# Weight loads split in halves, staged LN1 with transposes inside the projection, and a reordered attention-output phase in a fused linear-attention + ReGLU block

## The chip, the cores and the metric

The kernel runs on one core of a Trainium2 chip. The metric is device time in microseconds (us). "PE" is TensorE, "PEld" its weight loads, "DVE" VectorE, "ACT" ScalarE, "POOL" GpSimd, "SP" the sync engine, which here issues most loads. Each run lists the mean clock granted to TensorE over the whole run (1.0 is full speed).

## The reference, cut to what matters

```python
x = A_x                                             # 1 x 2048 x 1024, bf16
# block A: linear attention, 32 heads of 32
qkv = layernorm(x) @ wqkv ; pq, pk = phi(q), phi(k) # phi(t) = t+1 if t>0 else exp(t), + 1e-6
kv = pk^T v ; z = sum(pk)
o  = (pq kv) / (pq z + 1e-6)
h  = x + o @ wo
# block B: gated ReGLU, F = 3584
g  = relu(layernorm(h) @ W_gate) ; h2 = h + (g * (layernorm(h) @ W_up)) @ W_down
```

## The kernel before

All tensors are cut into 16 row tiles (`t`) of 128 rows. Every operation is recorded by a small scheduler, `E(engine, fn, reads, writes)`, which derives semaphore waits from the named buffers; each engine then runs its own list in the order of recording. PSUM has eight banks, handed out least recently used first (`alloc_banks`). The head of the kernel normalises four tiles, transposes each, and projects it with the first quarter of wkv:

```python
load_x(0, 1, halves=True)
load_x(1, 1)
load_wkv(jorder[0], "sp")            # 1 MB, one DMA
for t_ in range(2, 4): load_x(t_, 1)
...
def LN1(t, fast):                    # DVE: bn_stats x2, bn_aggr, +eps ; POOL: rstd = pow(-0.5)
    ...                              # fast: DVE normalises the tile; else POOL does, in two operations
def T1(t, eng="act"):                # 8 PE transposes into one bank, one eviction of 128x1024
    bk = transposes(ln1tile[t % N_L1], b_ln1tile[t % N_L1])
    t_evac(bk, lnT, b_ln1T[t], t, eng)
def KV(t, j):                        # 8 matmuls 128x512, then V's eviction (ACT) or phi (ACT, DVE, DVE)
    ...
for i in range(10):                  # warm-up matmuls on ident and etmp
    E("pe", ... e.matmul(psum[wb][:], lhsT=ident, rhs=etmp[0], ...))
LN1(blk0[0], True)
T1(blk0[0], "dve")
for idx, t in enumerate(blk0):       # the first four tiles
    if idx + 1 < len(blk0):
        LN1(blk0[idx + 1], idx + 1 < 2)
    KV(t, jorder[0])
    if idx + 1 < len(blk0):
        T1(blk0[idx + 1])
```

Later, "phase 4" computes the attention output, the projection with wo and the second layernorm in a software pipeline over tiles:

```python
for i in range(n_iter):
    if i < NT: ND(i)                 # PE: numerators and denominators, 3 banks
                                     # ACT: 3 x denominators + eps; DVE: reciprocal, 3 x normalise
    ... two Q projections while any are left (i < 8) ...
    if 0 <= i - 1 < NT: TO(i - 1)    # PE transposes, ACT eviction
    if 0 <= i - 2 < NT:
        for n in range(DC): A(i - 2, n)   # PE 2 x 8 matmuls; DVE adds the residual (eviction + row sums)
        LN2(i - 2)                   # ACT Square over the tile of h; DVE small; POOL rstd and normalise
    if i >= NT: ... two gate/up tasks GU ...
    if 0 <= i - TL_LAG < NT: TL(i - TL_LAG)  # TL_LAG = 4; PE transposes, ACT eviction
load_wd(); ...                       # then the dense gate/up and down projections, to the end
```

(The second block is shortened to its calls.)

## Time and profile before

| | before |
|---|---|
| time, median of the first 6 runs | 865.8 us (864.47 to 867.95) |
| span of the profiled run, its clock | 863.8 us, 0.998 |
| first useful projection matmul | 9.85 us |
| PE dense from | 21.8 us |
| period of a phase-4 iteration without Q | 5.83 us |
| weight loads waiting for the normalise line | 8.1 us |

From the page of the profiled run, the busy times (us, share of the span, instructions) and the engine shares of the chain that ended last:

```profile
PE 843.2 (98%) x4279; PEld 400.9 (46%) x4362; DVE 278.8 (32%) x541; ACT 193.5 (22%) x337; POOL 62.7 (7%) x101
...
PE 87%; DVE 5%; ACT 4%; DMA 3%; issue 1%; SPq 0%
```

TensorE is the engine that counts. In the timeline eight 128x512 matmuls take 1.727 us when nothing stops them, 0.216 us each; the kernel has 3712 of them, so some 801 us of its 864 cannot be touched by reordering. The Trainium skill (Perfetto Trace Analysis, "Identifying the Most-Contended Engine") warns that matmul busy time is no good measure of the distance to the limit. One must look for stretches in which the matmuls don't follow each other every 0.216 us. There are two.

**The head.** Lines of the timeline of the kernel before (start us, duration us, engine, line, operation, output<-input, count, and in brackets the idle time of the engine before it and what ended it). L502 is the projection, L483 the eviction of a transposed tile on ACT, L509 the eviction of V on ACT:

```profile
9.85 3.32 PE L502 MATMUL ps<-big 128*128 128x512 bf16 x8 [2.74 <-DMA big<-in_A_wqkv_dram]
...
13.21 0.60 ACT L509 ACTIVATE big<-ps 128x512 bf16<-128x512 f32 x1 [10.93 <-PE ps L502]
...
13.70 1.02 ACT L483 ACTIVATE big<-ps 128x1024 bf16<-128x1024 bf16 x1
...
14.78 1.90 PE L502 MATMUL ps<-big 128*128 128x512 bf16 x8 [1.16 <-ACT big L483]
...
18.51 1.67 PE L502 MATMUL ps<-big 128*128 128x512 bf16 x7 [1.38 <-ACT big L483]
...
21.79 8.81 PE L502 MATMUL ps<-big 128*128 128x512 bf16 x39 [1.16 <-ACT big L483]
```

The first projection starts at 9.85 us, when wkv has landed, and needs 3.32 us for eight matmuls. Then PE waits each time for two evictions in a row on ACT (0.60 and 1.02 us), because the next tile is transposed only after the whole projection, and V's eviction is ahead of it in ACT's list. (The line at 18.51 us shows seven matmuls of eight: one record is missing. Its first weight load, at 18.28 us, gives the start, so these tiles follow each other every 3.5 us.) From 21.79 us on the matmuls are dense. Stretches of 1 us of the same trace (length in us, busy PE us, number of matmuls, granted clock, DMA share, GB/s) show why the first eight were slow:

```profile
9.00:10.00 1.00, 0.15 (x1) 0.69 1.07 387
10.00:11.00 1.00, 1.00 (x3) 0.50 1.09 376
11.00:12.00 1.00, 1.00 (x4) 0.50 1.11 367
12.00:13.00 1.00, 1.00 (x4) 0.61 1.06 370
```

The clock fell to half. The warm-up matmuls had ended at 6.2 us and the first tile's transposes at 7.1 us; after that PE was idle.

**Phase 4 without Q.** One turn in the timeline of the kernel before (L564 normalise, L580 eviction of A, L586 Square, L483 eviction of TL's transposes, L552 denominators, L554 reciprocal, all on DVE or ACT; on PE L540 the ND matmuls, L475 the transposes of TO):

```profile
234.34 1.61 DVE L564 TENSOR_TENSOR big<-ps,rden 128x384 bf16<-128x384 f32 x3
...
235.54 0.29 PE L540 MATMUL ps<-big 128*128 128x132 bf16 x2 [0.24 <-DVE big L564]
235.86 0.68 DVE L580 SCALAR_TENSOR_TENSOR big<-ps,big 128x512 bf16<-128x512 f32 x1
...
236.00 0.62 PE L475 MATMUL ps<-big 128*128 128x128 bf16 x8 [0.17 <-DVE big L564]
...
236.47 0.69 DVE L580 SCALAR_TENSOR_TENSOR big<-ps,big 128x512 bf16<-128x512 f32 x1
...
237.20 1.06 ACT L586 ACTIVATE big<-big 128x1024 bf16<-128x1024 bf16 x1 [2.36 <-DVE big L580]
...
238.25 1.00 ACT L483 ACTIVATE big<-ps 128x1024 bf16<-128x1024 bf16 x1
...
239.16 0.59 ACT L552 ACTIVATE deneps<-ps 128x12 f32<-128x12 f32 x3
...
239.78 0.35 DVE L554 RECIPROCAL rden<-deneps 128x32 f32<-128x32 f32 x1 [1.24 <-ACT deneps L552]
...
240.16 1.61 DVE L564 TENSOR_TENSOR big<-ps,rden 128x384 bf16<-128x384 f32 x3
```

Follow the DVE and ACT lines from top to bottom: each starts where the one above ends, and the last is the first one again, 5.82 us later. It is a ring. PE itself needs only 4.8 us per iteration and is held up twice by the normalise (the brackets). The list of waits (us in total, times, longest) has for the weight loads over the whole run:

```profile
PEld ps L540 <- DVE big L564: 4.2, 13, 0.4
...
PEld ps L475 <- DVE big L564: 3.9, 8, 1.5
```

Together 8.1 us. The matmuls' own waits on that line (2.5 + 1.5 us) show only half of it: matmuls are pipelined, and the modelled end of the last one covers a part of the gap.

### The profile page before, as it was taken

To read this page: it belongs to the slowest core of one execution; us is meant where nothing else is said; L and a number is where in the kernel's file an instruction comes from. 1 tells how busy PE (TensorE), PEld (TensorE's weight loads), DVE (VectorE), ACT (ScalarE), POOL (GpSimd) and SP (SyncE) were. 2 spreads that over 40 slices of the span, in tenths; PEclk is the share of its full clock that TensorE was granted. 3 is DMA by queue.
4 is the path that set the end of the run, shared out by engine and by line. 5 is a ranking of instruction groups with operands and counts; after the bars stand their busy time and mean duration, and the time that the engine had idled before them with its cause. 6 is when DMAs were issued, how large, how long until landed. Compare 5 with 4: busy or idle time off the path is not lost.

```text
span 863.8 us, 10251 instructions
## 1 busy us (share of the span) xinstructions
PE 843.2 (98%) x4279; PEld 400.9 (46%) x4362; DVE 278.8 (32%) x541; ACT 193.5 (22%) x337; POOL 62.7 (7%) x101
## 2 busy tenths in 40 slices
PE   6999999999999999999999999999999999999998
PEld 2444446455544444444444444444444444444443
DVE  5465637887665211111112111111221011112101
ACT  2444432344565321100011110001111001111100
POOL 4123100012233000000000000000000000000000
PEclk9999999999999999999999999999999999999999
DMA  9500003700000469930055552025555103553000
GB/s 310 177 1 2 1 1 104 189 1 1 2 1 1 127 198 347 250 107 25 19 152 158 154 154 77 24 61 147 153 159 154 41 25 104 147 146 97 7 19 24
DMA packets 134413, 83.50 MB, mean 97 GB/s; under 512 B 2656, under 2 KB 127840, under 8 KB 134368
## 3 DMA queue, kind: packets, MB, share of 16 engines
q1 hardware_dynamic: 134224, 82.72, 32.4%
q8 instruction: 34, 0.56, 0.3%
q10 hardware_dynamic: 144, 0.13, 0.0%
q14 instruction: 11, 0.09, 0.0%
HBM read 78.64 MB, written 4.19 MB: 96 GB/s over the span
## 4 chain that ended last, share of the span: by engine, by line
PE 87%; DVE 5%; ACT 4%; DMA 3%; issue 1%; SPq 0%
PE ps L740 22%; PE ps L722 21%; PE ps L726 21%; PE ps L502 13%; PE ps L528 5%; DVE big L564 2%; PE ps L576 2%; DMA big<-in_B_W_gate_dram 2%; DVE big L580 2%; ACT big L483 1%; ACT big L586 1%; PE ps L475 1%; DMA big<-in_A_wqkv_dram 1%; PE ps L517 1%; ACT deneps L552 1%
## 5 line engine op out<-in xcount | busy, mean ns | idle before, releaser
L722 PE MATMUL ps<-big 128*128 128x512 bf16 x879 | 210.0, 379 | 1.2 <-DMA big<-in_B_W_gate_dram 0.3
L726 PE MATMUL ps<-big 128*128 128x512 bf16 x878 | 210.1, 379 | 0.9
L740 PE MATMUL ps<-big 128*128 128x512 bf16 x878 | 192.9, 379 | 0.9
L731 DVE TENSOR_TENSOR big<-ps,big 128x512 bf16<-128x512 f32 x112 | 77.4, 691 | 308.4 <-PE ps L726 308.4
L730 ACT ACTIVATE big<-ps 128x512 bf16<-128x512 f32 x112 | 66.8, 597 | 453.1 <-PE ps L722 453.1
L740 PEld LDWEIGHTS ps<-big 128*128 128x128 bf16 x896 | 87.7, 98 | 105.7
L726 PEld LDWEIGHTS ps<-big 128*128 128x128 bf16 x896 | 87.7, 98 | 105.7 <-DMA big<-in_B_W_up_dram 0.3
L722 PEld LDWEIGHTS ps<-big 128*128 128x128 bf16 x896 | 87.5, 98 | 105.5 <-DMA big<-in_B_W_gate_dram 0.8
L502 PE MATMUL ps<-big 128*128 128x512 bf16 x500 | 113.3, 382 | 7.0 <-ACT big L483 3.7
L502 PEld LDWEIGHTS ps<-big 128*128 128x128 bf16 x512 | 49.6, 98 | 64.7 <-ACT big L483 4.0
L744 DVE TENSOR_TENSOR big<-ps,big 128x512 bf16<-128x512 f32 x32 | 22.1, 691 | 171.3 <-PE ps L740 171.3
L494 DVE TENSOR_SCALAR big<-ps 128x512 bf16<-128x512 f32 x64 | 44.1, 689 | 59.1 <-ACT big L493 59.1
L528 PE MATMUL ps<-big 128*128 128x512 bf16 x251 | 56.4, 379 | 0.3
L576 PE MATMUL ps<-big 128*128 128x512 bf16 x243 | 55.9, 379 | 0.7
L493 ACT ACTIVATE big<-ps 128x512 bf16<-128x512 f32 x64 | 38.2, 597 | 68.6 <-PE ps L528 34.8
L483 ACT ACTIVATE big<-ps 128x1024 bf16<-128x1024 bf16 x47 | 47.5, 1015 | 6.3 <-PE ps L475 6.3
L496 DVE SCALAR_TENSOR_TENSOR big<-big 128x512 bf16<-128x512 bf16 x64 | 44.3, 692 | 2.2
L528 PEld LDWEIGHTS ps<-big 128*128 128x128 bf16 x256 | 24.7, 98 | 28.1
L576 PEld LDWEIGHTS ps<-big 128*128 128x128 bf16 x256 | 24.4, 98 | 26.4
L475 PE MATMUL ps<-big 128*128 128x128 bf16 x384 | 29.2, 219 | 2.7 <-DVE big L564 2.5
L475 PEld LDWEIGHTS ps<-big 128*128 128x128 bf16 x384 | 24.6, 98 | 13.8 <-DVE big L564 3.9
L509 ACT ACTIVATE big<-ps 128x512 bf16<-128x512 f32 x32 | 19.2, 599 | 45.2 <-PE ps L502 45.2
(44 smaller groups left out, 232.1 us busy)
## 6 DMA issues: line engine op xcount, KB each, us to landing
big<-in_B_W_gate_dram SPq DMA_DIRECT2D x56, 512.0 KB, 3.9
big<-in_B_W_up_dram SPq DMA_DIRECT2D x56, 512.0 KB, 4.8
big<-in_B_W_down_dram SPq DMA_DIRECT2D x4, 1792.0 KB, 17.2
big<-in_A_wqkv_dram SPq DMA_DIRECT2D x6, 1024.0 KB, 10.9
out_dram<-big SPq DMA_DIRECT2D x32, 128.0 KB, 1.7
big<-in_A_x_dram SPq DMA_DIRECT2D x6, 512.0 KB, 11.1
big<-in_A_wo_dram SPq DMA_DIRECT2D x1, 2048.0 KB, 8.5
big<-in_A_x_dram SPq DMA_DIRECT2D x3, 256.0 KB, 8.2
```

Source lines behind the costliest of these rows:

```text
L475: E("pe", lambda e, k=k: e.transpose(psum_bf[bk][:, k * P:(k + 1) * P], src_ap[:, k * P:(k + 1) * P], ident), reads=[src_buf, b_ident], wr ...
L483: E("act", lambda e: e.activation(dst, src, ACT.Copy), reads=[b_ps[bk]], writes=[dst_buf])
L494: E("dve", lambda e: e.tensor_scalar(ttmp[r], psum[bk][:], 0.0, 1e-6, op0=ALU.max, op1=ALU.add), reads=[b_ps[bk]], writes=[b_ttmp[r]])
L496: E("dve", lambda e: e.scalar_tensor_tensor(dst_ap, etmp[r], 1.0, ttmp[r], op0=ALU.min, op1=ALU.add), reads=[b_etmp[r], b_ttmp[r]], writes ...
L502: E("pe", lambda e, k=k: e.matmul(psum[bk][:], lhsT=lnT[:, k, t * P:(t + 1) * P], rhs=wkv[:, k, j * 512:(j + 1) * 512], start=(k == 0), st ...
L528: E("pe", lambda e, k=k: e.matmul(psum[bk][:], lhsT=wq[:, k, f * P:(f + 1) * P], rhs=lnT[:, k, c * 512:(c + 1) * 512], start=(k == 0), sto ...
L576: E("pe", lambda e, k=k: e.matmul(psum[bk][:], lhsT=oT[:, k, ts_ * P:(ts_ + 1) * P], rhs=wo[:, k, n * 512:(n + 1) * 512], start=(k == 0), ...
L722: E("pe", lambda e, k=k: e.matmul(psum[gb][:], lhsT=wgs[slot][:, k, fo:fo + P], rhs=lnT[:, k, c * 512:(c + 1) * 512], start=(k == 0), stop ...
L726: E("pe", lambda e, k=k: e.matmul(psum[ub][:], lhsT=wus[slot][:, k, fo:fo + P], rhs=lnT[:, k, c * 512:(c + 1) * 512], start=(k == 0), stop ...
L730: E("act", lambda e: e.activation(relu[r], psum[gb][:], ACT.Relu), reads=[b_ps[gb]], writes=[b_relu[r]])
L731: E("dve", lambda e: e.tensor_tensor(hhT[:, f, :], psum[ub][:], relu[r], op=ALU.mult), reads=[b_ps[ub], b_relu[r]], writes=[b_hh[f]])
L740: E("pe", lambda e, f=f: e.matmul(psum[bk][:], lhsT=hhT[:, f, tt * P:(tt + 1) * P], rhs=wd[:, f, n * 512:(n + 1) * 512], start=(f == 0), s ...
```

## The change

Its intent: get PE dense earlier, and take the bubbles out of phase 4. The diff, cut to its core; the lines of phase 4 are written without their range tests:

```diff
-    TL_LAG = 4
+    TL_LAG = 5
+    SQ_LAG = 3
@@ loads: wkv in two DMAs per quarter; x2 and x3 go to ACT's queue
+        KH = 2 if KT >= 2 else 1
+        b_wkv = [[Buf(f"wkv{j}_{h}") for h in range(KH)] for j in range(2 * DC)]
-            load_x(1, 1)
+            load_x(1, 1, q="sp")
+            load_x(2, 1, q="act")
         load_wkv(jorder[0], "sp")
-        for t_ in range(2, min(4, NT)):
-            load_x(t_, 1)
+            load_x(3, 1, q="act")
@@ warm-up: needs only DVE's memset; 12 ahead, 3 after the first transposes
-        NWARM = 10
-              ... e.matmul(psum[wb][:], lhsT=ident, rhs=etmp[0], ...)
+              ... e.matmul(psum[wb][:], lhsT=etmp[0][:, 0:P], rhs=etmp[0], ...)
+        warm(12)
@@ T1(split=True): two banks of four transposes, two ACT evictions; KV(mid=...): calls mid() after four matmuls
-        LN1(blk0[0], True)
-        T1(blk0[0], "dve")
+        ...
+        T1(blk0[0], "act", split=True)
+        warm(3)
         for idx, t in enumerate(blk0):
-            if idx + 1 < len(blk0):
-                LN1(blk0[idx + 1], idx + 1 < 2)
-            KV(t, jorder[0])
-            if idx + 1 < len(blk0):
-                T1(blk0[idx + 1])
+            if nx is not None:
+                for i in range(0 if idx == 0 else 1, DC):
+                    LN1_bn(nx, i)
+                LN1_fin(nx)
+                if nx2 is not None:
+                    LN1_bn(nx2, 0)           # statistics of the tile after next, while POOL computes rstd
+                LN1_norm(nx, True)           # on DVE for all four tiles
+                KV(t, jorder[0], mid=(lambda nx=nx: T1(nx, "act", split=True)))
+            else:
+                KV(t, jorder[0])
@@ phase 4
         for i in range(n_iter):
             ND(i)
-            Q, Q
-            TO(i - 1)
-            A(i - 2, 0); A(i - 2, 1); LN2(i - 2)
-            GU, GU                            # i >= NT
-            TL(i - 4)
+            TL(i - 5)
+            TO(i - 1)
+            Q or GU                           # GU from i >= NT - 1
+            A(i - 2, 0)
+            LN2(i - 3)
+            Q or GU
+            A(i - 2, 1)
```

More of the change, by code (lines that the diff above doesn't have):

```diff
@@ L329, in bass_sequential_preLN__linear_attn_block__glu_gated_reglu__prompt_kernel @@
         b_ln2T = bl("ln2T", NT)
-        b_wkv = bl("wkv", 2 * DC)
+        KH = 2 if KT >= 2 else 1
+        b_wkv = [[Buf(f"wkv{j}_{h}") for h in range(KH)] for j in range(2 * DC)]
         b_wq = bl("wq", DC)
@@ L381, in alloc_banks @@
             return got
+        E("dve", lambda e: e.memset(etmp[0], 0.0), writes=[b_etmp[0]])
         E("pool", lambda e: e.memset(mhalf[:], -0.5), writes=[b_mhalf])
@@ L387, in bass_sequential_preLN__linear_attn_block__glu_gated_reglu__prompt_kernel @@
                                             base=0, channel_multiplier=1), reads=[b_ident], writes=[b_ident])
-        E("pool", lambda e: e.memset(etmp[0], 0.0), writes=[b_etmp[0]])
         E("pool", lambda e: e.memset(vext[:, :, :, 128:129], 1.0), writes=[b_vones])
@@ L394, in bass_sequential_preLN__linear_attn_block__glu_gated_reglu__prompt_kernel, with load_x @@
             E("dve", lambda e, h=h: e.memset(mask4[32 * h:32 * h + 32, h:h + 1], 1.0), writes=[b_mask4])
-        def load_x(t0, m, q="sp", halves=False):
+        def load_x(t0, m, q="sp", halves=False, extra=()):
             if halves:
@@ L402, in load_x, with load_wkv, load_wq @@
                            writes=[b_x[t0][n]])
-                return
+                return None
             s_ = dsem()
             src = x2[t0 * P:(t0 + m) * P, :].rearrange("(t p) d -> p t d", p=P)
-            Sd.dma(q, lambda e: e.dma_start(xh[:, t0:t0 + m, :], src), s_,
-                   writes=[b for t in range(t0, t0 + m) for b in b_x[t]])
-        def load_wkv(j, q="act"):
-            s_ = dsem()
-            src = A_wqkv[:, D + j * 512:D + (j + 1) * 512].rearrange("(k p) n -> p k n", p=P)
-            Sd.dma(q, lambda e: e.dma_start(wkv[:, :, j * 512:(j + 1) * 512], src), s_, writes=[b_wkv[j]])
-        def load_wq(j, q="act"):
+            return Sd.dma(q, lambda e: e.dma_start(xh[:, t0:t0 + m, :], src), s_,
+                          writes=[b for t in range(t0, t0 + m) for b in b_x[t]], extra_waits=list(extra))
+        def load_wkv(j, q="sp", extra=(), halves=None):
+            tk_ = None
+            for h in (range(KH) if halves is None else halves):
+                s_ = dsem()
+                k0, k1 = h * KT // KH, (h + 1) * KT // KH
+                src = A_wqkv[k0 * P:k1 * P, D + j * 512:D + (j + 1) * 512].rearrange("(k p) n -> p k n", p=P)
+                tk_ = Sd.dma(q, lambda e, k0=k0, k1=k1, src=src: e.dma_start(wkv[:, k0:k1, j * 512:(j + 1) * 512], src), s_,
+                             writes=[b_wkv[j][h]], extra_waits=list(extra))
+            return tk_
+        def load_wq(j, q="act", extra=()):
             s_ = dsem()
             src = A_wqkv[:, j * 512:(j + 1) * 512].rearrange("(k p) n -> p k n", p=P)
-            Sd.dma(q, lambda e: e.dma_start(wq[:, :, j * 512:(j + 1) * 512], src), s_, writes=[b_wq[j]])
+            return Sd.dma(q, lambda e: e.dma_start(wq[:, :, j * 512:(j + 1) * 512], src), s_, writes=[b_wq[j]],
+                          extra_waits=list(extra))
         def load_wo(q="sp"):
@@ L428, in bass_sequential_preLN__linear_attn_block__glu_gated_reglu__prompt_kernel @@
         if NT > 1:
-            load_x(1, 1)
+            load_x(1, 1, q="sp")
+        if NT > 2:
+            load_x(2, 1, q="act")
         load_wkv(jorder[0], "sp")
-        for t_ in range(2, min(4, NT)):
-            load_x(t_, 1)
+        if NT > 3:
+            load_x(3, 1, q="act")
         t0 = min(4, NT)
@@ L447, in bass_sequential_preLN__linear_attn_block__glu_gated_reglu__prompt_kernel, with LN1_bn, LN1_fin @@
         phi_ring = Ring([0, 1])
-        def LN1(t, fast):
-            for i in range(DC):
-                E("dve", lambda e, i=i: e.bn_stats(stats1[:, t, i, :], xh[:, t, i * 512:(i + 1) * 512]),
-                  reads=[b_x[t][i]], writes=[b_stats1[t]])
+        def LN1_bn(t, i):
+            E("dve", lambda e: e.bn_stats(stats1[:, t, i, :], xh[:, t, i * 512:(i + 1) * 512]),
+              reads=[b_x[t][i]], writes=[b_stats1[t]])
+        def LN1_fin(t):
             E("dve", lambda e: e.bn_aggr(mv1[:, t, :], stats1[:, t].rearrange("p a b -> p (a b)")),
@@ L458, in LN1, with LN1_norm @@
               reads=[b_veps1[t], b_mhalf], writes=[b_rstd1[t]])
+        def LN1_norm(t, fast):
             r = t % N_L1
@@ L470, in LN1 @@
                   reads=b_x[t] + [b_nmr1[t], b_rstd1[t]], writes=[b_ln1tile[r]])
+        def LN1(t, fast):
+            for i in range(DC):
+                LN1_bn(t, i)
+            LN1_fin(t)
+            LN1_norm(t, fast)
         def transposes(src_ap, src_buf):
@@ L485, in t_evac, with T1 @@
                 E("dve", lambda e: e.tensor_copy(dst, src), reads=[b_ps[bk]], writes=[dst_buf])
-        def T1(t, eng="act"):
-            bk = transposes(ln1tile[t % N_L1], b_ln1tile[t % N_L1])
-            t_evac(bk, lnT, b_ln1T[t], t, eng)
+        def T1(t, eng="act", split=False):
+            src_ap = ln1tile[t % N_L1]
+            src_buf = b_ln1tile[t % N_L1]
+            if not split or KT < 2:
+                bk = transposes(src_ap, src_buf)
+                t_evac(bk, lnT, b_ln1T[t], t, eng)
+                return
+            h = KT // 2
+            for part in range(2):
+                bk = alloc_banks(1)[0]
+                ks = list(range(part * h, (part + 1) * h if part == 0 else KT))
+                for k in ks:
+                    E("pe", lambda e, k=k, bk=bk, k0=ks[0]: e.transpose(psum_bf[bk][:, (k - k0) * P:(k - k0 + 1) * P],
+                                                                        src_ap[:, k * P:(k + 1) * P], ident),
+                      reads=[src_buf, b_ident], writes=[b_ps[bk]], inc=(k == ks[-1]))
+                src = psum_bf[bk][:, 0:len(ks) * P].rearrange("p (k s) -> p k s", k=len(ks))
+                dst = lnT[:, ks[0]:ks[-1] + 1, t * P:(t + 1) * P]
+                E("act", lambda e, src=src, dst=dst: e.activation(dst, src, ACT.Copy), reads=[b_ps[bk]], writes=[b_ln1T[t]])
         def phi_evac(bk, dst_ap, dst_buf):
@@ L497, in phi_evac, with KV @@
               reads=[b_etmp[r], b_ttmp[r]], writes=[dst_buf])
-        def KV(t, j):
+        def KV(t, j, mid=None):
             bk = alloc_banks(1)[0]
             for k in range(KT):
+                if mid is not None and k == KT // 2:
+                    mid()
                 E("pe", lambda e, k=k: e.matmul(psum[bk][:], lhsT=lnT[:, k, t * P:(t + 1) * P],
                                                 rhs=wkv[:, k, j * 512:(j + 1) * 512], start=(k == 0), stop=(k == KT - 1)),
-                  reads=[b_ln1T[t], b_wkv[j]], writes=[b_ps[bk]], inc=(k == KT - 1))
+                  reads=[b_ln1T[t], b_wkv[j][k * KH // KT]], writes=[b_ps[bk]], inc=(k == KT - 1))
             if j < DC:
@@ L616, in bass_sequential_preLN__linear_attn_block__glu_gated_reglu__prompt_kernel, with warm @@
         wb = alloc_banks(1)[0]
-        NWARM = 10
-        for i in range(NWARM):
-            E("pe", lambda e: e.matmul(psum[wb][:], lhsT=ident, rhs=etmp[0], start=True, stop=True),
-              reads=[b_ident, b_etmp[0]], writes=[b_ps[wb]], inc=(i == NWARM - 1))
+        def warm(n):
+            for i in range(n):
+                E("pe", lambda e: e.matmul(psum[wb][:], lhsT=etmp[0][:, 0:P], rhs=etmp[0], start=True, stop=True),
+                  reads=[b_etmp[0]], writes=[b_ps[wb]], inc=(i == n - 1))
+        warm(12)
         NJ = 2 * DC
@@ L625, in bass_sequential_preLN__linear_attn_block__glu_gated_reglu__prompt_kernel @@
         blk0 = blocks[0]
-        LN1(blk0[0], True)
-        T1(blk0[0], "dve")
-        for idx, t in enumerate(blk0):
-            if idx + 1 < len(blk0):
-                LN1(blk0[idx + 1], idx + 1 < 2)
-            KV(t, jorder[0])
-            if idx + 1 < len(blk0):
-                T1(blk0[idx + 1])
+        nb0 = len(blk0)
+        for i in range(DC):
+            LN1_bn(blk0[0], i)
+        LN1_fin(blk0[0])
+        LN1_norm(blk0[0], True)
+        T1(blk0[0], "act", split=True)
+        warm(3)
+        for idx, t in enumerate(blk0):
+            nx = blk0[idx + 1] if idx + 1 < nb0 else None
+            nx2 = blk0[idx + 2] if idx + 2 < nb0 else None
+            if nx is not None:
[8 more added lines that the diff above has]
+                KV(t, jorder[0])
         for b, blk in enumerate(blocks):
@@ L651, in bass_sequential_preLN__linear_attn_block__glu_gated_reglu__prompt_kernel @@
                     T1(t_)
-        handoff(b_wkv, [b for row in b_pq for b in row])
+        handoff([b for row in b_wkv for b in row], [b for row in b_pq for b in row])
         q_tasks = [(f, c) for c in range(NCH) for f in range(KT)]
@@ L693, in bass_sequential_preLN__linear_attn_block__glu_gated_reglu__prompt_kernel @@
             handoff([b_ln1T[t]], [b_ln2T[t]])
-        n_iter = NT + TL_LAG + 1
+        n_iter = NT + max(TL_LAG, SQ_LAG) + 1
         q_rest = len(q_tasks) - qi
@@ L762, in bass_sequential_preLN__linear_attn_block__glu_gated_reglu__prompt_kernel, with q_some, gu_some @@
         gi = 0
+        def q_some(n_):
+            nonlocal qi
+            for _ in range(n_):
+                if qi < len(q_tasks):
+                    Q(*q_tasks[qi])
+                    qi += 1
+        def gu_some(n_):
+            nonlocal gi
+            for _ in range(n_):
+                if gi < len(gu_tasks) and gu_tasks[gi][0] == 0 and all(b_ln2T[t_].written for t_ in range(4)):
+                    GU(*gu_tasks[gi])
+                    gi += 1
         for i in range(n_iter):
+            q_now = q_per_iter if (qi < len(q_tasks) and i < q_iters) else 0
+            g_now = 2 if (i >= NT - 1 and gi < len(gu_tasks) and gu_tasks[gi][0] == 0) else 0
             if i < NT:
                 ND(i)
-            if qi < len(q_tasks) and i < q_iters:
-                for _ in range(q_per_iter):
-                    if qi < len(q_tasks):
-                        Q(*q_tasks[qi])
-                        qi += 1
+            if 0 <= i - TL_LAG < NT:
+                TL(i - TL_LAG)
             if 0 <= i - 1 < NT:
                 TO(i - 1)
+            q_some((q_now + 1) // 2)
+            gu_some((g_now + 1) // 2)
             if 0 <= i - 2 < NT:
-                t = i - 2
-                for n in range(DC):
-                    A(t, n)
-                LN2(t)
-            if i >= NT and gi < len(gu_tasks) and gu_tasks[gi][0] == 0:
-                for _ in range(2):
-                    if gi < len(gu_tasks) and gu_tasks[gi][0] == 0 and all(b_ln2T[t_].written for t_ in range(4)):
-                        GU(*gu_tasks[gi])
-                        gi += 1
-            if 0 <= i - TL_LAG < NT:
-                TL(i - TL_LAG)
+                A(i - 2, 0)
+            if 0 <= i - SQ_LAG < NT:
+                LN2(i - SQ_LAG)
+            q_some(q_now // 2)
+            gu_some(g_now // 2)
+            if 0 <= i - 2 < NT:
+                for n in range(1, DC):
+                    A(i - 2, n)
         while qi < len(q_tasks):
```

## The prediction

> **What bounds it now.** TensorE. The page gives PE 98% busy, PE 87% of the chain that ended last. In the timeline eight 128x512 matmuls pass in 1.727 us (0.216 us each) almost everywhere; 3712 of them are about 801 us, and nothing in the change removes one. Only idle or slow PE time can be won, and it lies in two places.
>
> 1. *Head, 0 to 22 us.* The timeline shows the first useful projection matmuls at 9.85 us, 2.7 us after PE went idle, released by the DMA of wkv (list of waits; 8.0 us in the chain). These eight take 3.3 us instead of 1.73 (granted clock 0.72 at 10-15 us). Then the chain goes round per row tile: matmuls, V eviction on ACT (0.60), transposed-tile eviction on ACT (1.02), next matmuls: starts at 14.78, 18.5, 21.79, about 3.5 us each, PE busy half. Dense from 21.8 us.
> 2. *Phase 4 without Q, 224 to 271 us.* The period is 5.83 us, though PE needs 3.45 (A) + 2x0.44 (transposes) + 0.4 (ND) = 4.73. The ring is DVE normalise (1.5) -> two A evictions (1.35) -> ACT Square (1.05) -> ACT TL eviction (0.9) -> ACT denominators (0.6) -> reciprocal (0.35) -> next normalise. PE's weight loads wait on that normalise 4.2+3.9 = 8.1 us in all (waits); about 0.5 + 6x1.05 + 1.5 us. Iterations with Q have period 8.27 against 8.2 needed: no gain there.
>
> **What changes.** Head: wkv comes in halves; x2, x3 move to ACT's queue; warm-up needs only DVE's memset, is two longer, with three more after the first transposes; tiles 2, 3 are normalised on DVE (0.55) instead of POOL (0.26+1.20); transposes are put into the middle of the preceding projection, so their eviction overlaps its second half, and V's eviction comes after it. Estimate from the durations: first projection at about 8.5 us at full clock, then about 2.75 us per tile (transposes 0.45, eviction 1.25, half a projection 0.86, latencies 0.2): last of the four starts at about 16.7 instead of 21.8. **Gain 5 us (3 to 7)**. The added warm-up costs nothing useful. The skill (TensorE: Matmul & The Clock Gate, "What's actually happening") says that the clock is released after some 3.4 us of activity and lost after an idle window; the slow first eight agree. The skill (DMA: Bandwidth & Descriptors, "Issuing engines are not separate DMA queues") says a second issuer adds no bandwidth, so loads still move at the 330-365 GB/s of 5-15 us and wkv's half cannot come very early.
>
> Phase 4: Square moves one iteration later, after both tile evictions on ACT, so A's last eviction is no longer in the ring. ACT needs about 3.9 us, DVE about 3.8 per iteration, under PE's 4.73. The bubble goes; gate/up work also fills iteration 15 and after. **Gain 8 us (6 to 8.5)**, all on the critical path, as PE runs densely afterwards. The w_down load keeps 14 gate/up tasks (48 us) before its use, against the 26 us it took: no new wait.
>
> **Time:** 865.8 - 5 - 8 = 852.7 us, range 849.5 to 858.0. Faster by over 2% (under 848.5): 0.06; within: 0.93; slower: 0.01.
>
> **What would show it.** Waits of PE weight loads on the normalise line near zero; phase 4 period near 4.75 us; projection dense from 16-17.5 us; clock 1.0 from 8 us; FFN cadence unchanged; the one gate-load wait at 343 us still under 1 us.
>
> **What would make it wrong.** Half of wkv lands no earlier, as the ACT queue's x loads share the engines; x2 late stalls DVE's statistics in front of tile 1's normalise; DVE, now waiting for Square before A's second eviction, holds a PSUM bank (7 of 8 used per iteration) and leaves part of the bubble.

## The result, and the profile after

The changed kernel took 852.12 us (median of 7 runs, 851.83 to 852.56), the kernel before 865.53 us (16 runs, 863.72 to 867.95). The ratio is 0.9846 (95% interval 0.9835 to 0.9858). Here and below a ratio is the mean time of one kernel's fast runs over that of the other's of the same rounds, so it is not quite the ratio of the medians quoted. The gain is 13.4 us, 1.5%: within 2%. The same two lines of the page, after:

```profile
PE 839.5 (99%) x4283; PEld 400.8 (47%) x4367; DVE 282.8 (33%) x543; ACT 195.8 (23%) x342; POOL 59.4 (7%) x96
...
PE 98%; DMA 1%; issue 1%; ACT 0%; SPq 0%; DVE 0%; ACTq 0%
```

PE's busy time hardly moved; the span did, and nearly all of the chain that ended last is now PE.

**The head** in the timeline after (L538 projection, L518 split transposes, L523 their evictions on ACT):

```profile
8.33 1.02 PE L538 MATMUL ps<-big 128*128 128x512 bf16 x4 [0.65 <-DMA big<-in_A_wqkv_dram]
...
9.39 0.62 PE L518 MATMUL ps<-big 128*128 128x128 bf16 x8
...
9.83 1.28 ACT L523 ACTIVATE big<-ps 128x512 bf16<-128x512 bf16 x2 [1.69 <-PE ps L518]
...
9.94 1.02 PE L538 MATMUL ps<-big 128*128 128x512 bf16 x4
...
11.17 1.04 PE L538 MATMUL ps<-big 128*128 128x512 bf16 x4 [0.20 <-ACT big L523]
...
13.80 1.04 PE L538 MATMUL ps<-big 128*128 128x512 bf16 x4 [0.28 <-ACT big L523]
...
16.44 8.81 PE L538 MATMUL ps<-big 128*128 128x512 bf16 x39 [0.28 <-ACT big L523]
```

The first half of the projection starts at 8.33 us and runs at full speed; the next tile's transposes stand between its halves, and ACT evicts them (from 9.83 us) while the second half runs. After the first, the tiles follow each other every 2.64 us, and PE is dense from 16.44 us instead of 21.79: 5.35 us. The first matmuls of phase 4 come by the same 5.34 us earlier, at 162.07 us instead of 167.41 us (first line before, second after):

```profile
167.41 0.63 PE L540 MATMUL ps<-big 128*128 128x132 bf16 x8
162.07 0.63 PE L576 MATMUL ps<-big 128*128 128x132 bf16 x8
```

The granted clock is 1.00 in every stretch from 6 to 17 us; one of them:

```profile
10.00:11.00 1.00, 0.96 (x5) 1.00 1.09 346
```

**Phase 4**, one turn after (on PE L576 ND, L494 the transposes of TL and TO together, L612 A; L588 denominators, L502 the two tile evictions on ACT, L600 normalise, L616 eviction of A, L622 Square):

```profile
228.27 0.63 PE L576 MATMUL ps<-big 128*128 128x132 bf16 x8
...
228.74 1.05 PE L494 MATMUL ps<-big 128*128 128x128 bf16 x16
...
229.43 1.94 ACT L502 ACTIVATE big<-ps 128x1024 bf16<-128x1024 bf16 x2
...
229.63 3.62 PE L612 MATMUL ps<-big 128*128 128x512 bf16 x16
229.96 1.61 DVE L600 TENSOR_TENSOR big<-ps,rden 128x384 bf16<-128x384 f32 x3
231.24 1.07 ACT L622 ACTIVATE big<-big 128x1024 bf16<-128x1024 bf16 x1
231.56 0.69 DVE L616 SCALAR_TENSOR_TENSOR big<-ps,big 128x512 bf16<-128x512 f32 x1
...
233.08 0.63 PE L576 MATMUL ps<-big 128*128 128x132 bf16 x8
```

ND starts at 228.27 and again at 233.08 us: 4.81 us, with no bracket on any PE line. Square (231.24) follows the tile evictions on ACT and waits for nobody; it even starts ahead of the eviction of A that DVE makes next to it, since it now works on the tile before. In the list of waits of this phase the weight loads no longer appear. From the start of phase 4 to the end the kernel is 13.5 - 5.34 = 8.2 us shorter (spans of 863.8 and 850.3 us): the 8.1 us of waits above.

### The profile page after: what moved, and what is told of

Its sections match the earlier page's. It is cut to its first block, busy times and chain, and to the rows that moved or that the text cites. A ratio compares the mean times of both kernels' runs of the same rounds, so it can differ in the third digit from the quotient of the medians.

```text
span 850.3 us, 10275 instructions
## 1 busy us (share of the span) xinstructions
PE 839.5 (99%) x4283; PEld 400.8 (47%) x4367; DVE 282.8 (33%) x543; ACT 195.8 (23%) x342; POOL 59.4 (7%) x96
## 4 chain that ended last, share of the span: by engine, by line
PE 98%; DMA 1%; issue 1%; ACT 0%; SPq 0%; DVE 0%; ACTq 0%
PE ps L791 23%; PE ps L773 23%; PE ps L777 23%; PE ps L538 13%; PE ps L612 6%; PE ps L564 6%; PE ps L494 2%; PE ps L576 1%; PE ps L553 1%; DMA big<-in_A_wqkv_dram 1%; ACT big L523 0%; PE ps L518 0%; DVE big L795 0%; SPq L408 0%; SPq L403 0%
## 5 line engine op out<-in xcount | busy, mean ns | idle before, releaser
L777 PEld LDWEIGHTS ps<-big 128*128 128x128 bf16 x896 | 87.7, 98 | 105.7
L791 PEld LDWEIGHTS ps<-big 128*128 128x128 bf16 x896 | 87.7, 98 | 105.7
L773 PEld LDWEIGHTS ps<-big 128*128 128x128 bf16 x896 | 87.4, 98 | 104.3
L538 PE MATMUL ps<-big 128*128 128x512 bf16 x500 | 112.4, 379 | 2.1 <-ACT big L523 0.8
L538 PEld LDWEIGHTS ps<-big 128*128 128x128 bf16 x512 | 49.1, 98 | 59.6 <-ACT big L523 3.4
L612 PE MATMUL ps<-big 128*128 128x512 bf16 x250 | 58.5, 379 | 0.3
L530 DVE SCALAR_TENSOR_TENSOR big<-big 128x512 bf16<-128x512 bf16 x64 | 47.5, 742 | 2.2
L502 ACT ACTIVATE big<-ps 128x1024 bf16<-128x1024 bf16 x44 | 43.5, 1022 | 13.1 <-PE ps L494 13.1
L612 PEld LDWEIGHTS ps<-big 128*128 128x128 bf16 x256 | 24.7, 98 | 28.6
L564 PEld LDWEIGHTS ps<-big 128*128 128x128 bf16 x256 | 24.6, 98 | 28.1
L600 DVE TENSOR_TENSOR big<-ps,rden 128x384 bf16<-128x384 f32 (+1 forms) x48 | 24.6, 513 | 1.7
L616 DVE SCALAR_TENSOR_TENSOR big<-ps,big 128x512 bf16<-128x512 f32 x32 | 22.0, 687 | 8.6 <-PE ps L612 8.5
```

Of the source, the lines that this page charges most:

```text
L502: E("act", lambda e: e.activation(dst, src, ACT.Copy), reads=[b_ps[bk]], writes=[dst_buf])
L530: E("dve", lambda e: e.scalar_tensor_tensor(dst_ap, etmp[r], 1.0, ttmp[r], op0=ALU.min, op1=ALU.add), reads=[b_etmp[r], b_ttmp[r]], writes ...
L538: E("pe", lambda e, k=k: e.matmul(psum[bk][:], lhsT=lnT[:, k, t * P:(t + 1) * P], rhs=wkv[:, k, j * 512:(j + 1) * 512], start=(k == 0), st ...
L564: E("pe", lambda e, k=k: e.matmul(psum[bk][:], lhsT=wq[:, k, f * P:(f + 1) * P], rhs=lnT[:, k, c * 512:(c + 1) * 512], start=(k == 0), sto ...
L612: E("pe", lambda e, k=k: e.matmul(psum[bk][:], lhsT=oT[:, k, ts_ * P:(ts_ + 1) * P], rhs=wo[:, k, n * 512:(n + 1) * 512], start=(k == 0), ...
L773: E("pe", lambda e, k=k: e.matmul(psum[gb][:], lhsT=wgs[slot][:, k, fo:fo + P], rhs=lnT[:, k, c * 512:(c + 1) * 512], start=(k == 0), stop ...
```

## The experiments

Each kernel ran on one chip together with runs of the kernel before. All outputs are right.

**The two parts alone.** The first is the changed kernel with the old phase-4 loop and `TL_LAG = 4`, the second the kernel before with the new loop:

```diff
# head_only: the changed kernel
-        for i in range(n_iter):  ... the new order ...
+        for i in range(n_iter):  ... the old order ...       # TL_LAG = 4, LN2(i - 2)
# p4_only: the kernel before
-        for i in range(n_iter):  ... the old order ...
+        for i in range(n_iter):  ... the new order ...       # TL_LAG = 5, SQ_LAG = 3
```

> The changed head (loads, warm-up, split transposes) with the old phase-4 loop. Theory: the two parts add, as TensorE is the only critical engine between them; head alone saves 5.3 us (dense projection from 16.4 us instead of 21.8), so about 860.2 us, and the old bubble stays: weight loads wait about 8 us on the normalise line, period 5.83 us. Rival: the parts overlap, an earlier head only moves a later wait; then under 3 us are saved here.

> The old head with the new phase-4 loop. Theory: saves 8.1 us, about 857.4 us; period 4.8 us in iterations without Q, weight loads wait under 1 us on the normalise line; the sum of the two savings is 13.4 us within 1 us. Rival (not additive): the sum differs by more than 2 us.

Measured: the head alone 860.07 us (5 runs, 859.94 to 860.31, all with clock 1.0), ratio 0.9950 (0.9938 to 0.9962). Phase 4 alone 856.58 us (6 runs, 855.44 to 859.71), ratio 0.9914 (0.9899 to 0.9930). The kernel before took 864.24 us there. The waits came out as foreseen: 8.1 us (4.2 + 3.9) on the normalise line with the old loop, none with the new one, whose period is 4.81 us. But against 864.24 us the savings, 4.2 and 7.7 us, add up to 11.9 and not 13.4 (the sum was expected within 1 us of it). What is missing is no interaction of the parts. It is the clock. 30 runs of the kernel before sort by granted clock, without overlap:

| granted clock | runs | time, us | mean, us |
|---|---|---|---|
| 1.000 | 8 | 863.22 to 863.90 | 863.68 |
| 0.998 | 14 | 863.93 to 865.75 | 864.96 |
| 0.996 | 3 | 865.95 to 866.62 | 866.29 |
| 0.994 | 5 | 867.01 to 867.70 | 867.34 |

(0.002 of 864 us is 1.7 us of full clock, that is about 3.5 us at half clock. The steps in mean time are less, 1.1 to 1.3 us; PE was idle during a part of the half clock, which in the profile above had begun before the first projection.) The two runs of phase 4 alone at clock 1.0 took 855.97 and 855.44 us, mean 855.7; two runs are few, but they lie 0.5 us apart. With full clock on both sides the head is worth 863.7 - 860.1 = 3.6 us, phase 4 863.7 - 855.7 = 8.0, and the changed kernel 863.7 - 852.1 = 11.6: the parts add. The other 1.8 us of the 13.4 are 865.5 - 863.7, the clock that the kernel before loses in most of its runs. What takes the second and third such piece in the runs at 0.996 and 0.994 is open: no profile fell on one of them.

**Which half of the phase-4 change breaks the ring?** `sq_lag_only` keeps the old order; `order_only` keeps the new order with LN2 in its old place.

```diff
# sq_lag_only: old loop (TL_LAG = 4), changed head
                 for n in range(DC):
                     A(t, n)
-                LN2(t)
+            if 0 <= i - 3 < NT:
+                LN2(i - 3)
# order_only: new loop, changed head
-            if 0 <= i - SQ_LAG < NT:
-                LN2(i - SQ_LAG)
             ...
                 for n in range(1, DC):
                     A(i - 2, n)
+                LN2(i - 2)
```

> Changed head, old order of phase 4, and only LN2 (with the Square) one iteration later. Theory: Square's dependence on A's second eviction of the same iteration is the link that closes the ring through ACT; without it nearly the whole bubble goes: period 4.8 us, about 852.5 us (within 1 us of the changed kernel). Rival: the position of the TL transposes and their eviction between Square and the denominators closes it; then the period stays above 5.3 us and the time above 856 us.

> Changed head, new order of phase 4 (TL first, Q and gate/up between the two halves of A), but LN2 not later: it follows A's second half in the same iteration. Theory: the ring keeps normalise 1.5, two A evictions 1.35, Square 1.05, denominators 0.6, reciprocal 0.35 = 4.9 us and loses the TL eviction; period about 5.0 us, so some 1.5 to 3 us slower than the changed kernel, 853.5 to 855 us. Rival (position is what counts): within 0.7 us of the changed kernel, period 4.8.

Measured: 851.97 us (4 runs, 851.88 to 852.15) and 852.35 us (4 runs, 851.95 to 852.64), all with clock 1.0. My expectation held for the first and fell for the second: each half alone gives nearly the whole gain. The timeline of `order_only` shows what I had missed. First Square on ACT, then ND on PE:

```profile
224.49 1.06 ACT L622 ACTIVATE big<-big 128x1024 bf16<-128x1024 bf16 x1 [1.45 <-DVE big L616]
...
229.41 1.06 ACT L622 ACTIVATE big<-big 128x1024 bf16<-128x1024 bf16 x1 [1.45 <-DVE big L616]
```

```profile
228.03 0.63 PE L576 MATMUL ps<-big 128*128 128x132 bf16 x8
...
232.85 0.63 PE L576 MATMUL ps<-big 128*128 128x132 bf16 x8
...
242.48 0.63 PE L576 MATMUL ps<-big 128*128 128x132 bf16 x8
...
247.40 0.63 PE L576 MATMUL ps<-big 128*128 128x132 bf16 x8
...
252.31 0.63 PE L576 MATMUL ps<-big 128*128 128x132 bf16 x8
```

The ring is still there and has the length I had added up: Square comes every 4.92 us and waits for A's eviction each time (in the changed kernel it does not). But PE turns every 4.81 us until 242.48 and follows the ring at 4.92 us only in the last two turns. The ring falls behind by 0.1 us per iteration, and for five iterations the slack between the producers and PE takes that up; then there are only two iterations left, which cost 0.2 us. The slack is thus some 0.5 us (an estimate: five times 0.1). The old ring of 5.83 us falls behind by 1.0 us per iteration: in the kernel before, the first TO after the Q projections (at 230.18 us) was late by 0.5 us, and the following ones by the full 1.0; here too 0.5 us of slack went first. My error was to compare periods only. What a ring costs is its lag times the iterations, less the slack.

**Where does the head's gain come from?** Four edits of the changed kernel, each taking one piece back:

```diff
# mid_off
-                KV(t, jorder[0], mid=(lambda nx=nx: T1(nx, "act", split=True)))
+                KV(t, jorder[0])
+                T1(nx, "act", split=True)
# loads_old
-        KH = 2 if KT >= 2 else 1
+        KH = 1
-            load_x(2, 1, q="act")
         load_wkv(jorder[0], "sp")
-            load_x(3, 1, q="act")
+        for t_ in range(2, min(4, NT)):
+            load_x(t_, 1)
# warm_short
-        warm(12)
+        warm(10)
-        warm(3)
# norm_pool
-                LN1_norm(nx, True)
+                LN1_norm(nx, idx + 1 < 2)
```

> The changed kernel, but the split transposes of the next tile come after the whole projection of this one instead of in its middle. Theory: the loop per tile is again projection 1.73, V eviction 0.6 ahead of the transposed tile's 1.28: about 3.5 us instead of 2.64, so the fourth tile starts near 19.3 us instead of 16.4 and the time is 2 to 3 us longer, 854.2 to 855.2 us. Rival (the gain of the head is the earlier data and the clock alone): under 0.7 us longer.

> The changed kernel with the old loads: wkv whole, x2 and x3 on SP's queue behind it. Theory: the first block of wkv lands near 9.7 us again instead of 8.2; the extra warm-up ends near 7.7, so PE idles about 2 us and keeps its clock; the four tiles start 1.5 us later, 853.3 to 854 us. Rival: LN1, not wkv, sets the start (the transposed tile is evicted only at 8.14 us), so the loads are worth under 0.5 us.

> The changed kernel with 10 warm-up matmuls ahead and none after the first transposes (as the kernel before has it in number). Theory: PE idle before the first projection is only about 1.5 us (6.85 to 8.33), shorter than the 2.9 us after which the kernel before ran at half clock, so little changes: clock 1.0, within 0.5 us. Rival: without the three extra matmuls the clock falls to 0.5 for about 3 us and the first tiles cost 1 to 1.5 us more.

> The changed kernel with tiles 2 and 3 normalised on POOL again. Theory: rstd to normalised tile takes 0.55 + 0.26 + 1.20 us and hand-overs, about 2.2 instead of 1.2 us; transposes of tiles 2 and 3 wait for it, about 1 us later each, but the second is partly hidden as statistics run ahead: 0.7 to 1.8 us longer, 852.8 to 853.9 us. Rival: the loop is bound by ACT's evictions (2 x 0.64 + V) and this costs nothing, within 0.3 us.

Measured (four runs each), against 851.95 us (851.70 to 852.19, four runs) of the changed kernel repeated on the same chip:

| taken back | runs, us | median, us | longer by, us |
|---|---|---|---|
| transposes in the middle (`mid_off`) | 855.64 to 855.99 | 855.84 | 3.9 |
| loads (`loads_old`) | 853.35, 854.76, 854.81, 855.14 | 854.79 | 2.8 |
| warm-up (`warm_short`) | 852.10, 853.69, 854.05, 854.17 | 853.87 | 1.9 |
| normalisation on DVE (`norm_pool`) | 852.43 to 852.85 | 852.53 | 0.6 |

*Transposes.* The timeline of `mid_off` has the old loop again:

```profile
12.65 1.90 PE L538 MATMUL ps<-big 128*128 128x512 bf16 x8 [1.42 <-ACT big L523]
...
16.41 1.90 PE L538 MATMUL ps<-big 128*128 128x512 bf16 x8 [1.42 <-ACT big L523]
...
20.18 6.00 PE L538 MATMUL ps<-big 128*128 128x512 bf16 x27 [1.42 <-ACT big L523]
```

The period is 3.76 us. It was expected at 3.5; in two pieces the eviction takes 1.28 us where the whole one took 1.02, so without the overlap the split alone is a loss, which is a part of the 3.9 us. That the time grew by 3.9 us, and not by the 2 to 3 expected, has this cause in part; and in this profile the second half of the first projection also waited 0.35 us for the second half of wkv. The place between the halves of the projection is the largest piece of the head.

*Loads.* The run at clock 1.0 took 853.35 us, 1.4 more than the changed kernel, as expected; the three at 0.998 took 854.76 to 855.14. I had expected the clock to hold. In the profiled run (clock 0.998) the first projection starts at 9.11 us, 0.8 us later than in the changed kernel. Then DVE stands still, because the statistics of tile 2, placed ahead of tile 1's normalisation, need x2, which is again behind wkv on SP's queue:

```profile
9.75 0.69 DVE L458 BATCH_NORM_STATS2 stats<-big 128x6 f32<-128x512 bf16 x1 [1.79 <-DMA big<-in_A_x_dram]
10.36 0.53 DVE L472 TENSOR_SCALAR big<-big,mv,rstd 128x1024 bf16<-128x1024 bf16 x1
```

The transposes come only at 10.95 us, after 0.82 us of waiting, and then the clock goes: 0.50 in the stretches from 11 to 14 us. PE had been idle from about 7.5 to 9.1 us and again before 10.95. So moving x2 to the other queue belongs together with the staged LN1, which would have run into this wait.

*Warm-up.* Three of four runs lost 1.7 to 2.2 us, one (852.10) next to nothing. In the profiled one (854.05 us, clock 0.998) two things add: the first half of wkv came later than in the changed kernel's profile (projection from 9.33 us instead of 8.33), with the same loads; and the clock was 0.50 from 10 to 13 us, so that the way from the first to the third tile took 6.47 us (9.33 to 15.80) where it takes 5.47 (8.33 to 13.80). My expectation (within 0.5 us) fell. That the three dummy matmuls after the first transposes carry the clock over is likely but not shown by this run alone: the edit also takes away two of the warm-up matmuls ahead, and in the profile PE waited 2.24 us for wkv where it waited 0.65 in the changed kernel. `before_warm` below adds dummies after the transposes and nothing else. One thing stays open: the run of 854.17 us is listed with clock 1.0, so its delay has another cause or the listed clock hides it. It can hide something: in every profile the weight loads of the warm-up matmuls follow each other every 0.43 us up to about 4 us, which is the spacing at clock 0.50 in the kernel before (10.23, 10.66, 11.09 us), and yet the clock of these stretches reads 1.00.

*Normalisation.* 0.6 us (all four runs above the four of the changed kernel), less than the 0.7 to 1.8 expected: only one of the two tiles waits. In the trace of `norm_pool` the third tile starts 3.09 us after the second, 0.45 more than in the changed kernel, but the fourth follows 2.64 us later as before.

Two pieces of the new head were not taken back alone: the earlier start of the warm-up (1.24 us instead of 1.91) and the eviction of the first tile, which went from DVE to ACT in two parts.

**The clock alone.** The kernel before with 12 dummy matmuls and nothing else:

```diff
         T1(blk0[0], "dve")
+        for i in range(12):
+            E("pe", lambda e: e.matmul(psum[wb][:], lhsT=ident, rhs=etmp[0], ...))
```

> The kernel before with 12 dummy matmuls after the first transposes (about 6.95 to 9.6 us) and nothing else. Theory: the half clock between about 9.7 and 12.5 us costs the first projection 3.3 us instead of 1.73; kept busy, PE keeps its clock: about 1.6 us faster, and the run-to-run spread falls from some 3 us to under 1 us, clock 1.0 in every run. Rival: the chain of transposes and evictions that follows absorbs it, no gain.

Measured: 863.45 us (6 runs, 863.09 to 864.38), every one with clock 1.0; the kernel before on that chip 865.44 us (863.56 to 867.70). The ratio is 0.9977 (0.9962 to 0.9993). The spread is 1.3 us, not under 1 as expected, by the one run at 864.38; the other five lie within 0.4 us. The time is that of the kernel before's own runs at clock 1.0 (863.68). The timeline of this run shows the dummies (L629) lead up to the first projection, which passes at full speed:

```profile
6.74 2.75 PE L629 MATMUL ps<-big 128*128 128x512 bf16 x12
9.33 1.89 PE L502 MATMUL ps<-big 128*128 128x512 bf16 x8
```

Useless work, in a place where PE had nothing to do, is worth 2.0 us (of the medians) to the kernel before.

**Can the remaining gaps be filled?** In the changed kernel PE still stands 0.2 to 0.45 us before the second, third and fourth tile, until ACT has evicted the transposes. `weave` puts second-row projections, whose inputs are ready, into these places:

```diff
+        ln_next(0); KV(blk0[0], jorder[0], mid=... T1(blk0[1]))
+        ln_next(1); KV(blk0[1], jorder[0], mid=... T1(blk0[2]))
+        ln_next(2)                         # weave2: + LN1(tile 4), LN1(tile 5) here
+        KV(blk0[0], jorder[1])
+        KV(blk0[2], jorder[0], mid=... T1(blk0[3]))
+        KV(blk0[1], jorder[1])
+        KV(blk0[3], jorder[0])
+        KV(blk0[2], jorder[1])
+        KV(blk0[3], jorder[1])             # weave2: + T1(tile 4), T1(tile 5) after it
```

> The changed kernel once more, on the same chip as the next run, so that the two compare: 852.1 us, head dense from 16.4 us, gaps of 0.2 to 0.45 us before each of the first four tiles (about 1.4 us of PE idle from 9 to 16.5 us).

> The changed kernel with the second row of projections (wkv block 0) of tiles 0 to 2 put between the first rows of tiles 1, 2, 3. Theory: PE is idle about 0.45 us before each tile because the transposed tile is still being evicted; other ready matmuls fill it: 0.8 to 1.4 us shorter, 850.7 to 851.3 us, if the second block of wkv lands by 13.5 us. Rival: that block lands later than 14 us and PE waits for it instead: same or slower by up to 1 us.

Measured: 852.59 us (4 runs, 852.39 to 852.79), 0.6 slower than the changed kernel beside it. The first theory fell, and the rival's reason is wrong too: no matmul waited for the second block of wkv. Tiles 4 and 5 had been moved a row later with the rest, and their normalisation on POOL was late:

```profile
33.19 0.62 PE L494 MATMUL ps<-big 128*128 128x128 bf16 x8 [1.02 <-POOL big L481]
```

`weave2` puts LN1 of these two tiles back ahead of the second row.

> The woven rows again, with the statistics and POOL normalisation of tiles 4 and 5 back where the changed kernel has them (in the first weave they came a row later and PE waited 1.0 us for POOL, then the fast runs were 852.4 to 852.8). Theory: filling the three gaps of 0.2 to 0.45 us before the tiles saves about 1 us: 850.8 to 851.5 us, PE waits on POOL zero. Rival: the saving is eaten by the phi evictions on DVE, 852 us or more.

Measured: 851.20 us (5 runs, 850.97 to 851.52), ratio to the kernel before 0.9836 (0.9817 to 0.9854). The time is as expected, the wait on POOL is gone, and the transposes of tiles 4 and 5 start at 24.07 us instead of 25.09. All five runs lie below all eleven of the changed kernel (851.70 to 852.56), though not on the same chip, and the intervals of the two ratios to the kernel before overlap. (At clock 1.0 the kernel before took 863.56 and 863.77 us on this chip and 863.59 on the other.) So this version beats the kernel before, and most likely the changed one by some 0.8 us; side by side the two did not run.

## Why the prediction was right

- *Time.* 852.7 us foretold, 852.12 measured; inside 849.5 to 858.0, and within 2%.
- *What bounds the kernel.* Right: PE only, and the gain is time in which it stood or ran at half clock. Busy PE time went from 843.2 to 839.5 us while the span lost 13.5.
- *Head, "Gain 5 us".* 5.35 in the profiled pair. "First projection at about 8.5 us at full clock", "about 2.75 us per tile", "last of the four starts at about 16.7": 8.33, 2.64 and 16.44. The start at 8.33 is partly luck: in the profiles with the new loads it lies between 8.13 and 9.33 us. The second issuer brought little bandwidth, as foretold: 362 GB/s from 5 to 15 us against 347 before. The 5.35 us hold for a kernel before that lost its clock; with full clock on both sides the head is worth 3.6. The largest piece is the transposes' place (3.9 us when taken back), then the loads (2.8, of which 1.4 without the loss of clock) and the warm-up (1.9). Taken back one by one the pieces come to 9.2 us, more than the whole: two of them bring about the same loss of clock, and the split eviction without its place is worse than the old one.
- *Phase 4, "Gain 8 us".* 8.0 alone at full clock, 8.2 in the profiled pair. DVE was busy 3.8 us per iteration as foretold (19.01 us in five), ACT 3.4 instead of 3.9. The period of 4.81 us (foretold "near 4.75 us"), the end of the waits, and the iterations with Q (8.27 us before and after) came as written.
- *The reason given for phase 4* was narrower than the truth. "A's last eviction is no longer in the ring" is what happens, but `order_only` shows that it isn't needed: with Square still in the ring the new order shortens it from 5.83 to 4.92 us, and PE feels 0.2 us of the rest. Nor was the new order needed: `sq_lag_only`, with the old one, takes 851.97 us. Either change by itself opens the ring far enough.
- *"The added warm-up costs nothing useful"* was right but too weak. I took the full clock as a consequence of the earlier load. With the three dummies and two of the warm-up matmuls taken away, three of four runs are slower by 1.7 to 2.2 us and two of these list a lower clock; with twelve dummies added the old head keeps its clock in all six runs. About 1.8 of the 13.4 us are this clock. It took both changes: `loads_old`, with all the dummies, lost it in three of four runs.
- *Named risks.* "x2 late stalls DVE's statistics" did not happen in the changed kernel, and did, as described, when the old loads were put back. The PSUM worry did not show. The w_down load ended without a wait on PE; the one small gate-load wait at 343 us, which I had expected to stay, is absent from the changed kernel's list of waits.

## What to carry to other kernels

When the busiest engine says 98%, look at its cadence and at the waits of its weight loads stage by stage: the lost time shows as a period longer than the engine's own work, and one link taken out of the ring of the other engines removes it; a ring that lags only a little costs nothing for some iterations. Put the producer's last step (here transposes and their eviction) into the middle of the consumer's previous work, not after it. In a head that waits for data keep TensorE busy with dummy matmuls right up to the first useful one, and compare versions at the same granted clock before believing a difference of one microsecond.

## What the Trainium skill lacked or had wrong

- TensorE: Matmul & The Clock Gate, "HAM oscillation": it gives the rule as no PE-idle gaps above about 3.4 us. Here a gap of some 2.7 us (7.1 to 9.85 us in the kernel before) was followed by a clock of 0.50 for about 3 us (it fell within the gap: the mean from 9 to 10 us is 0.69), and in `loads_old` gaps of 1.6 and 0.8 us were enough. But in `p4_only` a gap of 2.2 us and in `mid_off` three of 1.4 us left the clock at 1.00. So no bound on the length of a gap alone fits these traces. That the result varies from run to run, as the section "What's actually happening" says, agrees: the kernel before had clocks from 0.994 to 1.0 in 30 runs.
- The same page, "What's actually happening", puts the ramp below 1% of a typical kernel and advises against fitting a count of slow matmuls. It is small here too (means 1.3 to 3.7 us above the runs at clock 1.0, of 864), but it is 1.8 of the 13.4 us gained, and with it went most of the run-to-run spread (4.5 us over those 30 runs, 0.9 over eleven of the changed kernel).
- Perfetto Trace Analysis, "DMA Optimizations", says splitting a load may let some of the work start sooner. It did (projection at 8.33 us instead of 9.85), but the arrival is unsteady, which that section doesn't mention: with the split loads the first projection started between 8.13 and 9.33 us in ten profiles, with whole ones between 9.11 and 9.85 in four.
- No page that I read has the cost of a ring across engines: lag per iteration times iterations, less slack (4.92 against 4.81 us cost 0.2 us in all; 5.83 cost 1.0 us per iteration).
